# Two layers behind a linear attention: the second layer's weight loads planned as landing later, the weights' type change all on VectorE, first queries and keys loaded ahead of the first values

## The chip, the core and the metric

The program runs on one core of one Trainium2 chip. A time is the device time of one execution in microseconds (us), and of several runs the median. The engines are named as in the profile: PE (TensorE, the matmuls), DVE (VectorE), ACT (ScalarE), POOL (GpSimd; here it only issues DMAs that add to what lies in memory) and SP (SyncE, which issues all other DMAs, in order, each when what it waits for is done).

## The reference

Linear attention with decay over 2 batches, 8 heads, 768 positions of 64 values, and behind it two feed-forward layers on 1536 tokens (512 to 2048 to 512), the first with h·relu6(h+3)/6, the second with h·tanh(softplus(h)). All in fp32.

```python
for t in range(S):
    state = gamma * state + einsum('bhd,bhe->bhde', k[:, :, t], v[:, :, t])
    y[:, :, t] = scale * einsum('bhd,bhde->bhe', q[:, :, t], state)
x = y.transpose(0, 2, 1, 3).reshape(B * S, H * D)
h = x @ w_in;  g = h * clip(h + 3, 0, 6) / 6;    x = g @ w_out      # first layer
h = x @ w_in;  g = h * tanh(log1p(exp(h)));      out = g @ w_out    # second layer
```

## The kernel before, in words

**The work.** The attention goes by 12 units (6 chunks of 128 positions, 2 batches). A unit loads `qk` (queries and keys, 512 KB) and `kv` (keys, values and decay factors, 516 KB). On PE it has scores `sc`, the state's update `kv`, what the state gives `qv`, and what the chunk itself gives `pv`. Before `kv` the keys are multiplied by decay factors: `kp`, on DVE in one instruction (L600) or on ACT in eight (L598), as the letter of the unit in `KPD` says. The scores are multiplied by a mask (L612), which is made once from two tables (matmuls that read the loaded `rows`, tile `cvd`) and a triangle (`tri`) in L429; ACT copies five more tables to `qtab` (L435).

A layer is computed transposed, features on partitions and 512 tokens at a time, in three blocks. A product of fp32 accuracy is three passes of PE in its faster fp32 form: each operand is split into a high and a low part (high on ACT, L483 or L893; low on DVE, L485 or L895), and high·high, low·high and high·low are added in PSUM. Where pairs of blocks are multiplied, seven products stand for eight (as Strassen's do): the up products are named P1 to P7, of two blocks of tokens (`w`) or of the halves of one (`v`); DVE adds their sums in PSUM to what ACT copied (L850; the plan calls these c11, c12, c22), and a later product (P4) uses the bank that such an addition (c22) has read.

**The weights.** They lie in memory as 64-bit words. For each pair of feature tiles there are two loads of 1 MB (`raw`, L454): up weights (converted into tile `cvu`) and down weights (`cvd`). Of the two `raw` buffers a third load can take one only when the first has been converted. A conversion is four instructions, one behind the other: a shift (L468), a shift-and-or (L469), a mask (L471), and the top part, a change from fp32 to fp16 with a factor 0.5. This last one is on ACT (L474) or on DVE (L476), as the letter in `TOPS` says, two conversions a letter (first eight letters: the first layer's pairs; last eight: the second's). So ACT makes 24 of them before, each of 128x1024.

**The second layer's sums.** Products of different pairs of features are added in memory: the first time by a plain write from SP (L981, tile `part`), later by DMAs from POOL that add (L983).

**What sets the order.** Everything is first a list of tasks (`Plan.add`) with an engine, a duration, and what it depends on. `Plan.order` plays them through with the table of costs at the top of the file, and issues them in the order in which that play has them start; each engine then runs its own instructions strictly in that order, whatever the real times. `EARLY` gives the order of PE's attention tasks (s, k, q, b) and of the first layer's first up (h) and down (o) tasks; `LOADS` the first six loads. `Plan.lat` is what the plan adds after the end of a task before its successors may start: `DLAT` for what SP issues, 0.06 otherwise. `Plan.ranks` counts back from the tasks that PE needs, with the same latencies. So a larger latency for a load has two effects: its rank asks for it earlier, and the instructions that read it are placed later among their engine's others.

Of the kernel before, what the change touches and what calls it, by code (L numbers as in the profile page):

```python
# [44 lines left out]
LAT = 0.06  # L45
# [2 lines left out]
SC, KV, QV, PV = 0.86, 0.43, 0.42, 0.84  # L48
TURN = 0.15
LEAD = (7.2, 5.5)  # L50
EARLY = "bskbskkbbkqssqssbkqsqsqqkbskqkksqbbhqobqskbobhhhohohhohhshoohoooboho"
LOADS = "kv0 qk0 kv1 tri qk1 rows"
DLAT = 1.45
OUT = 4.0
COLD = 9.0
EARLY_Y = (1, 2, 5, 6, 3, 7, 4)
# [3 lines left out]
ORDER = (1, 5, 6, 3, 7, 2, 4)  # L60
AFTER = ("bp", "bp", "bp", "pb")
BORDER = {"pb": (2, 3, 0, 1), "bp": (0, 1, 2, 3)}
TOPS = "DDDDAAAAAAAAAAAA"
KPD = "ADDADDDADA"


def dve(n, two=True):
    return 0.15 + n * (1.045e-3 if two else 0.525e-3)


def act(n, bias=False):
    return 0.17 + n * 0.86e-3 + (0.09 if bias else 0.0)
# [30 lines left out]
class Plan:  # L103
# [3 lines left out]
    def add(self, nm, eng, dur, deps, bufs, emit, rank=None):  # L107
        bufs = list(dict.fromkeys(getattr(b, "base", b) for b in bufs))
        t = Task(nm, eng, dur, deps, bufs, emit, rank)
        t.idx = len(self.tasks)  # L110
        self.tasks.append(t)
        for b in bufs:
            if not b.users:
                t.new.append(b)
                b.owner = t
            elif b.owner not in t.deps:
                t.deps.append(b.owner)
            b.users.append(t)
        for d in t.deps:
            d.succ.append(t)  # L120
        return t

    @staticmethod
    def lat(d):
        return DLAT if d.eng == "SP" else LAT

    def ranks(self):
        for t in reversed(self.tasks):
# [79 lines left out]
def body(ctx: ExitStack, tc: tile.TileContext, aps: dict, out: bass.AP):  # L208
# [17 lines left out]
    def buf(pool, shape, tag, dt=F32):  # L226
        count[0] += 1
        name = f"{tag}_{count[0]}"

        def make():  # L230
            if pool == "post" and "post" not in pools:
                att.close()
                pools["post"] = ctx.enter_context(tc.tile_pool(name="post", bufs=1, reuse_waits="tile"))
            return pools[pool].tile(shape, dt, tag=tag, name=name, bufs=BUFS.get(tag, 1))
        return Buf(tag, make)
# [7 lines left out]
    V, A = nc.vector, nc.scalar  # L243
    pl = Plan()
    add = pl.add
# [26 lines left out]

    first = LOADS.split()
    cst, tri_b = buf("fix", [P, 1024], "cvd"), buf("att", [P, P], "tri")
# [98 lines left out]
    hq = i = 0  # L373
    for c in EARLY:
        if c in "skqb":
# [68 lines left out]
    def words_of(layer, p, half, cb, parts):  # L444

        rb = buf("fix", [P, 1024], "raw", I64)
        src = aps["w1" if layer == 0 else "w2"][p, half]

        def part(k):
            n = 1024 // parts  # L450
            cs = slice(k * n, (k + 1) * n)
            nm = f"w{layer}_{p}_{half}{k}"
            ld = add(nm, "SP", DMA512 * n / 512, [], [rb],
                     lambda: nc.sync.dma_start(out=rb.tile[:, cs], in_=src[:, cs]))  # L454
            ld.after = ld_w[0]
            ld_w[0] = ld

            def words():
                w = rb.tile.bitcast(I32).rearrange("p (n t) -> p n t", t=2)
                return w[:, cs, 0], w[:, cs, 1]  # L460

            def ci():
                return cb.tile.bitcast(I32)[:, cs]

            def top():
                return cb.tile.bitcast(F16).rearrange("p (n t) -> p n t", t=2)[:, cs, 1]
            a1 = add(nm + "l", "DVE", dve(n, False), [ld], [rb, cb],
                     lambda: V.tensor_scalar(ci(), words()[0], 29, None, ALU.logical_shift_right))  # L468
            a2 = add(nm + "o", "DVE", dve(n), [a1], [cb, rb], lambda: V.scalar_tensor_tensor(  # L469
                out=ci(), in0=words()[1], scalar=3, in1=ci(), op0=ALU.logical_shift_left, op1=ALU.bitwise_or))  # L470
            a3 = add(nm + "m", "DVE", dve(n, False), [a2], [rb], lambda: V.tensor_scalar(  # L471
                words()[1], words()[1], -0x2000, None, ALU.bitwise_and))
            if TOPS[8 * layer + p] == "A":
                return add(nm + "t", "ACT", act(n), [a3], [cb, rb], lambda: A.activation(  # L474
                    top(), words()[1].bitcast(F32), AF.Copy, scale=0.5))
            return add(nm + "t", "DVE", dve(n, False), [a3], [cb, rb], lambda: V.tensor_scalar(  # L476
                top(), words()[1].bitcast(F32), 0.5, None, ALU.mult))
        return part

# [96 lines left out]
    def unit(u):  # L576
# [15 lines left out]
        if c < NCH - 1:  # L592
            kpb = buf("att", [P, DM], "kp")

            def run_kp():
                for h in range(H):
                    hs = slice(h * D, (h + 1) * D)
                    A.activation(kpb.tile[:, hs], kb.tile[:, hs], AF.Copy, scale=kb.tile[:, 2 * DM + h:2 * DM + h + 1])  # L598
            if KPD[u] == "D":
                t_kp = add(f"kp{u}", "DVE", DVE1, [ld_kv[u]], [kb, kpb], lambda: V.tensor_tensor(  # L600
# [626 lines left out]
```

## Time and profile before

| | |
|---|---|
| median of 3 runs | 548.85 us (548.23 to 549.57) |
| profiled execution: its time, its span | 550.77 us, 549.0 us |
| PE busy | 537.0 us of the span |
| DVE busy | 441.2 us |
| ACT busy | 330.2 us |
| chain that ended last | PE 94%, DMA 3%, ACT 1%, issue 1% |

How to read the rows below: a time at the start of a row is in us from the start of the span. `out<-in` are tile names without their numbers; `x3` counts instructions. A bracket at a row's end is the idle time of the engine ahead of the instruction and what ended it. Granted clock 1.00 is PE at 2.4 GHz and 0.50 at 1.2 GHz. PE's matmuls overlap: one of 128x512 lasts 0.39 us, and one starts 0.227 us after the other when nothing holds them.

### The profile page before, as it was taken

Reading aid. Unit: us, or ns where it says so; the run is one execution under the profiler, and the core shown is the slowest. Engines: PE = TensorE matmul, PEld = TensorE weight load, DVE = VectorE, ACT = ScalarE, POOL = GpSimd, SP = SyncE. Lnnn points to the kernel's source line nnn. Section 1 sums busy time; section 2 is a strip of 40 time slices with the busy share of each in tenths; the row PEclk is TensorE's granted clock in tenths of the full one; section 3 lists DMA queues with packets and bytes.
Section 4 is the critical chain, followed back from the end, with each engine's and each line's share of the span. In section 5 each row is a group of like instructions: output and inputs, shape, how many; then the busy total and the mean of one; then the engine's idle time right before and its main releaser. Section 6 shows DMA issues by size and latency. Waiting matters only on the chain.

```text
span 549.0 us, 8237 instructions
## 1 busy us (share of the span) xinstructions
PE 537.0 (98%) x3142; PEld 452.5 (82%) x3143; DVE 441.2 (80%) x716; ACT 330.2 (60%) x572; POOL 31.9 (6%) x40
## 2 busy tenths in 40 slices
PE   7999999999999999999999999998999999999996
PEld 4888888888889988888888898876988898888985
DVE  3999999599746994678999989956899778878592
ACT  4666453566724644457655787764868776867440
POOL 0000000000000000000000000010023300540000
PEclk9999999999999999999999999997999999999999
DMA  8985522122400242003130023392259942995232
GB/s 310 369 289 205 214 83 92 72 77 78 153 1 1 76 155 77 1 5 137 35 133 0 1 88 141 116 266 80 78 123 191 190 111 76 146 143 173 79 127 102
DMA packets 19111, 65.79 MB, mean 120 GB/s; under 512 B 2128, under 2 KB 2512, under 8 KB 15232
## 3 DMA queue, kind: packets, MB, share of 16 engines
q1 hardware_dynamic: 13888, 55.83, 28.2%
q0 software_dynamic: 5184, 9.44, 11.7%
q8 instruction: 24, 0.39, 0.3%
q14 instruction: 15, 0.12, 0.1%
HBM read 49.53 MB, written 15.73 MB: 119 GB/s over the span
## 4 chain that ended last, share of the span: by engine, by line
PE 94%; DMA 3%; ACT 1%; issue 1%; DVE 0%; SPq 0%; DVEq 0%; ACTq 0%
PE acc L241 49%; PE wx L241 24%; PE wy L241 21%; DMA raw<-in_w_dram 2%; DMA qk<-in_qk_dram 1%; ACT cvd L474 0%; DVE g L850 0%; ACT qc L674 0%; ACT wbh L483 0%; SPq L260 0%; DVE cvu L468 0%; ACT sb L972 0%; ACT qc L972 0%; ACT t L972 0%; DVE xch L975 0%
## 5 line engine op out<-in xcount | busy, mean ns | idle before, releaser
L241 PE MATMUL acc<-gh,wdh 128*128 128x512 f32 x264 | 103.1, 390 | 0.0
L241 PE MATMUL acc<-gh,wdl 128*128 128x512 f32 x264 | 103.0, 390 | 0.0
L241 PE MATMUL acc<-gl,wdh 128*128 128x512 f32 x264 | 102.7, 389 | 0.0
L241 PEld LDWEIGHTS acc<-gl,wdh 128*128 128x128 f32 x264 | 49.6, 188 | 10.4
L241 PEld LDWEIGHTS acc<-gh,wdh 128*128 128x128 f32 x264 | 49.6, 188 | 9.8 <-issue 0.2
L241 PEld LDWEIGHTS acc<-gh,wdl 128*128 128x128 f32 x264 | 49.6, 188 | 9.3
L893 ACT CAST gh<-g 128x512 fp32r<-128x512 f32 x56 | 34.8, 621 | 28.9 <-PE acc L241 23.7
L895 DVE TENSOR_TENSOR gl<-g,gh 128x512 fp32r<-128x512 f32 x56 | 38.4, 687 | 15.3 <-ACT gh L893 12.9
L983 POOL DMA_DIRECT2D part<-sb x18 | 15.9, 955 | 440.2 <-ACT sb L972 426.1
L895 DVE TENSOR_TENSOR gl<-gs,gh 128x512 fp32r<-128x512 f32 x29 | 20.0, 688 | 12.2 <-ACT gh L893 11.2
L485 DVE SCALAR_TENSOR_TENSOR wdl<-cvd,wdh 128x512 fp32r<-128x512 f32 x32 | 21.7, 686 | 9.9 <-ACT wdh L483 9.7
L763 ACT ACTIVATE t<-g,bias 128x512 f32<-128x512 f32 (+1 forms) x22 | 14.6, 664 | 24.0 <-DVE g L850 21.0
L241 PE MATMUL acc<-gh,sb 128*128 128x512 f32 x92 | 28.3, 389 | 0.0
L893 ACT CAST gh<-gs 128x512 fp32r<-128x512 f32 x29 | 18.0, 621 | 14.6 <-PE acc L241 14.3
L483 ACT ACTIVATE wdh<-cvd 128x512 fp32r<-128x512 f32 x32 | 20.0, 637 | 6.9 <-PE acc L241 6.8
L531 DVE TENSOR_TENSOR cvu<-cvu 128x256 f32<-128x256 f32 x56 | 23.5, 420 | 0.5
L471 DVE TENSOR_SCALAR raw<-raw 128x1024 int32<-128x1024 int32 (+1 forms) x34 | 22.3, 657 | 0.0
L241 PE MATMUL wy<-xbh,wsh 128*128 128x512 f32 x56 | 22.3, 398 | 0.0
L241 PE MATMUL wy<-xbh,wsl 128*128 128x512 f32 x56 | 22.3, 398 | 0.0
L241 PE MATMUL wx<-q,wsh 128*128 128x512 f32 x56 | 21.8, 389 | 0.0
L850 DVE TENSOR_TENSOR g<-wy,g 128x512 f32<-128x512 f32 (+1 forms) x26 | 14.6, 564 | 8.5 <-PE wy L241 8.1
L485 DVE SCALAR_TENSOR_TENSOR wsl<-cvu,wsh 128x1024 fp32r<-128x1024 f32 x14 | 17.1, 1222 | 4.5 <-ACT wsh L483 4.4
(248 smaller groups left out, 1509.0 us busy)
## 6 DMA issues: line engine op xcount, KB each, us to landing
raw<-in_w_dram SPq DMA_DIRECT2D x30, 1024.0 KB, 4.8
kv<-in_kv_dram SPq DMA_DIRECT2D x12, 516.0 KB, 6.0
qk<-in_qk_dram SPq DMA_DIRECT2D x12, 512.0 KB, 6.3
part<-sb POOLq DMA_DIRECT2D x18, 256.0 KB, 5.0
raw<-in_w_dram SPq DMA_DIRECT2D x4, 512.0 KB, 9.4
part<-q POOLq DMA_DIRECT2D x8, 256.0 KB, 5.6
part<-sb SPq DMA_DIRECT2D x6, 256.0 KB, 2.1
part<-t POOLq DMA_DIRECT2D x5, 256.0 KB, 5.4
```

The source lines that it names most:

```text
L241: nc.tensor.matmul(o, l, r, start=start, stop=stop, skip_group_check=True)
L471: a3 = add(nm + "m", "DVE", dve(n, False), [a2], [rb], lambda: V.tensor_scalar(words()[1], words()[1], -0x2000, None, ALU.bitwise_and))
L483: lambda: A.activation(hb.tile[:, h0:h0 + n], cb.tile[:, c0:c0 + n], AF.Copy, scale=256.0))
L485: return add(nm + "lo", "DVE", dve(n), [a], list(dict.fromkeys([cb, hb, lb])), lambda: V.scalar_tensor_tensor(out=lb.tile[:, l0:l0 + n], i ...
L531: prev = [add(nm + f"s{o}", "DVE", dve(256), prev, [cb], lambda o=o, x=x, y=y, op=op: V.tensor_tensor(out=q(o), in0=q(x), in1=q(y), op=op))]
L763: lambda: A.activation(tb.tile[:, cs], src.tile[:, cs], AF.Relu, bias=bias3))
L850: return add(f"c{k}_{nm}", "DVE", dve(n), deps, [ps, gb], lambda: V.tensor_tensor(out=gb.tile[:, gc], in0=ps.tile[:, pc], in1=gb.tile[:, g ...
L893: a = add(f"hi{nm}", "ACT", act(512), deps + [prev_split[0]], [gb, gh], lambda: A.copy(gh.tile, gb.tile))
L895: lambda: V.tensor_tensor(out=gl.tile, in0=gb.tile, in1=f32(gh.tile), op=ALU.subtract))
L983: landed[tp] = added[b, d] = add(f"pa{nm}", "POOL", ADDED, [dep, added[b, d]], [tp, pt], lambda: nc.gpsimd.dma_start(out=pt.tile, in_=tp.t ...
```

## The change

Three things in the tables and rules of the plan; no instruction's own work is changed.

- `Plan.lat` gives the loads of the second layer's weights (task names that begin with `w1_`) 7.0 us to land instead of 1.45. All other loads keep 1.45.
- `TOPS` is `D` throughout: the 24 type changes that were on ACT are on DVE. The planned cost of one is 1.1 times the plan's formula on DVE (it was 1.0), and 1.33 times on ACT, where none is left.
- `EARLY` and `LOADS` are new, and one letter of `KPD`: the first loads are `rows`, `tri`, `qk` of unit 0, `kv` of units 0 and 1, `qk` of unit 1; `kp` of unit 6 is made on ACT in eight instructions instead of on DVE in one.

```diff
-EARLY = "bskbskkbbkqssqssbkqsqsqqkbskqkksqbbhqobqskbobhhhohohhohhshoohoooboho"
-LOADS = "kv0 qk0 kv1 tri qk1 rows"
-DLAT = 1.45
+EARLY = "bkssksqssqksbbkkqbkbsqbsqkqbkqksqkbhqbqsshobbhhohhhhkooosoohoohhboooh"
+LOADS = "tri rows qk0 kv0 kv1 qk1"
+DLAT, WLAT = 1.45, 7.0
...
-TOPS = "DDDDAAAAAAAAAAAA"
-KPD = "ADDADDDADA"
+TOPS = "DDDDDDDDDDDDDDDD"
+KPD = "ADDADDAADA"
...
-        return DLAT if d.eng == "SP" else LAT
+        return (WLAT if d.nm[:3] == "w1_" else DLAT) if d.eng == "SP" else LAT
...
-                return add(nm + "t", "ACT", act(n) * 1.33 ...
+...
```

Since the plan is played anew, every engine's order shifts. Two places are shown, before and after.

**The start, SP.** The first loads that SP issues, before (`kv_78` and `qk_85` are unit 0, `kv_87` and `qk_89` unit 1):

```order
L281 DMA cvd_76<-in_rows_dram 48x704
L260 DMA kv_78<-in_kv_dram 128x1032
L260 DMA tri_83<-in_tri_dram 128x128
L260 DMA qk_85<-in_qk_dram 128x1024
L260 DMA kv_87<-in_kv_dram 128x1032
L260 DMA qk_89<-in_qk_dram 128x1024
```

And now (`qk_83` and `kv_85` are unit 0):

```order
L281 DMA cvd_76<-in_rows_dram 48x704
L260 DMA tri_78<-in_tri_dram 128x128
L260 DMA qk_83<-in_qk_dram 128x1024
L260 DMA kv_85<-in_kv_dram 128x1032
L260 DMA kv_87<-in_kv_dram 128x1032
L260 DMA qk_89<-in_qk_dram 128x1024
```

The first values have gone from second place to fourth, the triangle and the first queries and keys are each one place further ahead. `rows` stays first.

**The start, ACT.** Its first instructions after loading its table, before: the decayed keys of unit 0 (eight), then the tables, then the first copies of the state (`st`).

```order
L598 ACTIVATE kp_103<-kv_78 128x64 x8
L435 COPY qtab_133<-wy_99 128x512
L435 COPY qtab_135<-wx_112 128x512
L435 COPY qtab_137<-acc_40_118 128x512
L435 COPY qtab_139<-acc_41_121 128x512
L624 COPY st_156<-acc_34_80 128x512
```

And now:

```order
L435 COPY qtab_110<-wy_101 128x512
L435 COPY qtab_114<-wx_106 128x512
L435 COPY qtab_118<-acc_40_112 128x512
L435 COPY qtab_130<-acc_41_116 128x512
L598 ACTIVATE kp_132<-kv_85 128x64 x8
L435 COPY qtab_150<-acc_42_145 128x512
```

Four tables have moved ahead of `kp`, which waits for the values.

**The second layer's first sums, DVE.** The instructions around the first one that reads the up weights of the second layer's pair 4 (`cvu<-raw`, L468), before; the L850 rows are the additions c11, c12 and c22 of pair 2's up products:

```order
L850 TENSOR_TENSOR g_739_3530<-wy_3586,g_739_3530 128x512
L485 SCALAR_TENSOR_TENSOR wdl_3608<-cvd_3370,wdh_3599 128x512
L468 TENSOR_SCALAR cvu_3611<-raw_3566 128x1024
L850 TENSOR_TENSOR g_740_3595<-wy_3557,g_740_3595 128x512
L531 TENSOR_TENSOR cvd_3370<-cvd_3370 128x256
L850 TENSOR_TENSOR g_742_3582<-wx_3409,g_742_3582 128x512
```

And now (the L850 rows of 128x256 are the additions of the next set of products, pair 2's `v`):

```order
L850 TENSOR_TENSOR g_740_3604<-wy_3573,g_740_3604 128x512
L485 SCALAR_TENSOR_TENSOR wdl_3630<-cvd_3460,wdh_3618 128x512
L850 TENSOR_TENSOR g_742_3592<-wx_3545,g_742_3592 128x512
L485 SCALAR_TENSOR_TENSOR wdl_3648<-cvd_3460,wdh_3627 128x512
L531 TENSOR_TENSOR cvd_3460<-cvd_3460 128x256 x4
L850 TENSOR_TENSOR wsh_753_3582<-wy_3661,wsh_753_3582 128x256
L850 TENSOR_TENSOR wsh_753_3582<-wy_3633,wsh_753_3582 128x256
L485 SCALAR_TENSOR_TENSOR sb_263_3678<-cvd_3460,sb_263_3678 128x1024
L468 TENSOR_SCALAR cvu_3698<-raw_3580 128x1024
L850 TENSOR_TENSOR wsh_753_3582<-wx_3559,wsh_753_3582 128x256
```

The reader of the load stood between c11 and c12 of pair 2; it now stands behind all three of them, behind two of the next set, the sums of the down weights (L531) and their split (L485).

**The same place, SP.** The load that this reader waits for is `raw_274`; before:

```order
L981 DMA part20_331_3484<-sb00_696_3325 128x512
L981 DMA part21_332_3491<-sb01_697_3334 128x512
L454 DMA raw_265_3515<-in_w2_dram 128x1024
L454 DMA raw_274_3566<-in_w2_dram 128x1024
L981 DMA part12_329_3570<-q_695_3406 128x512
L981 DMA part13_330_3574<-q_695_3406 128x512
```

And now:

```order
L981 DMA part20_331_3475<-sb00_696_3328 128x512
L981 DMA part21_332_3486<-sb01_697_3338 128x512
L981 DMA part12_329_3552<-q_695_3411 128x512
L981 DMA part13_330_3556<-q_695_3411 128x512
L454 DMA raw_265_3569<-in_w2_dram 128x1024
L454 DMA raw_274_3580<-in_w2_dram 128x1024
```

The two loads now stand behind the two writes of sums that followed them.

## Rows read from the trace of the kernel before

**Rows 1.** The page's first part: busy time, share of the span, instructions

```profile
PE 537.0 (98%) x3142; PEld 452.5 (82%) x3143; DVE 441.2 (80%) x716; ACT 330.2 (60%) x572; POOL 31.9 (6%) x40
```

**Rows 2.** Waits of PE: in total, times, longest (us)

```profile
PE wx L241 <- DVE g L850: 4.0, 1, 4.0
PE wy L241 <- DMA qk<-in_qk_dram: 2.0, 1, 2.0
```

**Rows 3.** Timeline of PE around its longest wait: start, duration, instruction

```profile
368.87 0.39 PE L241 MATMUL wx<-xal,wbh 128*128 128x512 f32 x1
373.23 0.80 PE L241 MATMUL wx<-t4h,wbh 128*128 128x512 f32 x1 [3.98 <-DVE g L850]
...
378.93 0.39 PE L241 MATMUL wx<-t2h,wsl 128*128 128x512 f32 x1
```

**Rows 4.** Windows there: busy time of each engine, granted clock, DMA share

```profile
373.23:378.88 5.65, 5.65 (x13) 4.46 (x14) 2.69 (x5) 3.06 (x5) 0.00 (x0) 0.50 0.00 0
378.88:384.50 5.62, 5.62 (x27) 4.63 (x26) 3.93 (x5) 3.25 (x5) 0.00 (x0) 1.00 0.52 187
```

**Rows 5.** Timeline of DVE around PE's longest wait

```profile
370.95 0.69 DVE L468 TENSOR_SCALAR cvu<-raw 128x1024 int32<-128x1024 int32 x1 [4.20 <-DMA raw<-in_w_dram]
...
372.49 0.69 DVE L850 TENSOR_TENSOR g<-wx,g 128x512 f32<-128x512 f32 x1
```

**Rows 6.** The chain that ended last, there: start, us, what

```profile
361.85 9.01 DMA raw<-in_w_dram
```

**Rows 7.** Timeline of SP there: two issues, from the first to the second's end

```profile
356.92 5.27 SPq L454 DMA_DIRECT2D raw<-in_w_dram  x2
```

**Rows 8.** Timeline of POOL there, first and last of four

```profile
355.94 1.01 POOL L983 DMA_DIRECT2D part<-sb  x1 [355.49 <-ACT sb L972]
...
360.90 1.23 POOL L983 DMA_DIRECT2D part<-qc  x1
```

**Rows 9.** The page's DMA issues: times, KB each, median us to landing

```profile
raw<-in_w_dram SPq DMA_DIRECT2D x30, 1024.0 KB, 4.8
```

**Rows 10.** A group of instructions by form: busy, mean ns of one, idle before

```profile
L474 ACT ACTIVATE cvu<-raw 128x1024 f16<-128x1024 f32 x12 | 16.6, 1386 | 0.8 <-DVE raw L471 0.7
```

**Rows 11.** Instructions of L476: duration ns min/median/max, first and last start

```profile
L476 DVE TENSOR_SCALAR cvu<-raw x5: 458/756/760, 19.1 to 93.8; 128x1024 f16<-128x1024 f32 x3, 128x512 f16<-128x512 f32 x2
```

**Rows 12.** A window where DVE is full, columns as in rows 4

```profile
290.00:310.00 20.00, 19.99 (x88) 16.23 (x87) 20.00 (x34) 12.74 (x22) 0.00 (x0) 1.00 0.00 0
```

**Rows 13.** Timeline of PE at the start

```profile
5.17 1.06 PE L241 MATMUL acc<-cvd 48*128 48x512 bf16 x2
8.27 0.55 PE L241 MATMUL wy<-qk 64*128 64x128 f32 x1 [2.04 <-DMA qk<-in_qk_dram]
...
9.04 0.42 PE L241 MATMUL wy<-qk 64*128 64x128 f32 x1
...
9.26 0.42 PE L241 MATMUL wy<-qk 64*128 64x128 f32 x1
...
10.28 1.12 PE L241 MATMUL acc<-kv,kp 128*64 128x64 f32 x16
...
13.01 0.63 PE L241 MATMUL wy<-qk 64*128 64x128 f32 x2
...
15.72 0.27 PE L241 MATMUL wy<-qk 64*128 64x128 f32 x1
...
15.84 0.27 PE L241 MATMUL wy<-qk 64*128 64x128 f32 x1
...
18.05 0.43 PE L241 MATMUL acc<-qs,st 64*64 64x128 f32 x2
```

**Rows 14.** Timeline of ACT and DVE at the start: what the first loads release

```profile
4.58 2.02 ACT L598 ACTIVATE kp<-kv 128x64 f32<-128x64 f32 x8 [2.56 <-DMA kv<-in_kv_dram]
...
4.82 0.69 DVE L429 TENSOR_TENSOR mask<-wy,tri 128x512 f32<-128x512 f32 x1 [3.38 <-DMA tri<-in_tri_dram]
```

**Rows 15.** The chain that ended last, at the start

```profile
2.12 6.02 DMA qk<-in_qk_dram
```

More of the change, by code (lines that the diff above doesn't have):

```diff
@@ L50 @@
 LEAD = (7.2, 5.5)
-EARLY = "bskbskkbbkqssqssbkqsqsqqkbskqkksqbbhqobqskbobhhhohohhohhshoohoooboho"
-LOADS = "kv0 qk0 kv1 tri qk1 rows"
-DLAT = 1.45
+EARLY = "bkssksqssqksbbkkqbkbsqbsqkqbqksqkbhqbqsshobbhhohhhhkooosoohoohhboooh"
+LOADS = "tri rows qk0 kv0 kv1 qk1"
+DLAT, WLAT = 1.45, 7.0
 OUT = 4.0
@@ L473, in part @@
             if TOPS[8 * layer + p] == "A":
-                return add(nm + "t", "ACT", act(n), [a3], [cb, rb], lambda: A.activation(
+                return add(nm + "t", "ACT", act(n) * 1.33, [a3], [cb, rb], lambda: A.activation(
                     top(), words()[1].bitcast(F32), AF.Copy, scale=0.5))
-            return add(nm + "t", "DVE", dve(n, False), [a3], [cb, rb], lambda: V.tensor_scalar(
+            return add(nm + "t", "DVE", dve(n, False) * 1.1, [a3], [cb, rb], lambda: V.tensor_scalar(
                 top(), words()[1].bitcast(F32), 0.5, None, ALU.mult))
```

## The prediction

> **What bounds the kernel now.** I read the page's busy times first, then PE's waits, then the places that these named in the timeline. PE is busy 537.0 of 549.0 us [rows 1]: what does not shorten PE's idle time, or raise its clock, is worth nothing. Its waits hold two entries of any size [rows 2]: 4.0 us once, for an addition on DVE, and 2.0 us once, for the first queries and keys. The 4.0 us are in the second layer: no matmul starts between 368.87 and 373.23 [rows 3]. DVE is named as the releaser, but DVE itself stood still there for 4.20 us, waiting for a weight load [rows 5]; PE's addition (L850, 372.49) was queued behind that load's first reader, with which it has nothing to do. The load took 9.01 us from issue to landing [rows 6], where the median of its kind is 4.8 [rows 9]. In these 9 us POOL's four adding DMAs, issued from 355.94 on [rows 8], shared the DMA engines with it and with the 1 MB load issued 4.9 us ahead of it [rows 7].
>
> The stall costs twice. For 5.65 us behind it PE's granted clock is 0.50, the lower of its two levels, and 13 matmuls take what 27 do at 1.00 [rows 4]. From 368.87 to 378.93 there are 14 steps from one matmul to the next [rows 3]; at 0.227 us each they need 3.2 us. So 10.06 - 3.2 = 6.9 us went there: 4.1 standing, 2.8 on the clock.
>
> **The change, part by part.**
>
> *The longer landing time.* It takes the reader of that load (L468) out of the way. DVE came to it at 366.75 (370.95 less the wait, [rows 5]), just behind c11 of pair 2. In the new order it stands behind c12, c22 and two additions of the `v` products, so PE does three more products of 512 columns and four of 256 first: 18 x 0.227 + 24 x 0.12 (half of 0.227, and some) = 7.0 us, and DVE the 128x1024 split behind them, some 1.2 us. DVE asks at about 375. SP issues both loads together, when the conversions ahead are done, now on DVE: about 362 to 363, for the second load was already issued at 361.85, when ACT had finished the same conversion. That is 12 to 13 us of room. Landing: at best twice 2.6 us of transfer and some 2 us beside it (4.8 less 2.6), 7 us; at worst the 9.01 us of before and the other load's 2.6 us ahead of it, 11.6. It lands in time by either end, though by only half a microsecond or so at the worst. Gain 6.9 us; both ends are kept (6.9, or a stall of a few us left over). Past it, the second layer's other loads landed within the times that the old order allowed, since PE's waits name no other; the new order asks for all of them later after their issue.
>
> The two loads are also moved behind two SP writes of 256 KB. These wait for ACT's copies of the last products' sums, finished at about the same time as the conversions; cost 0, at worst 1 us off the room above.
>
> The Trainium skill ("DMA: Bandwidth & Descriptors", Queues, rings and completion order) says that each DMA engine takes turns, packet by packet, between the queues that have work for it. The trace agrees as far as it goes: 9.01 us beside POOL's queue, 4.8 without. By that rule two loads in one queue share one turn; with all of POOL's four still running they would take 2 x 5.1 us and 2 of latency, 12.2, at the edge of that room.
>
> *The type change on DVE.* 24 x 0.756 = 18.1 us are added to DVE's 441.2 [rows 1, 11] and 24 x 1.386 = 33.3 us leave ACT (12 of them have the row in [rows 10], the 12 for `cvd` take the same). Neither is on the chain: DVE goes from 80% to 84% of the span. What hides it is DVE's own idle time, 549 - 441 = 108 us. Where there is none it would show: from 290 to 310 DVE is busy for all of 20 us, and PE still never waits [rows 12]. The new order moves no conversion into that stretch. A chain of a conversion gets shorter (0.756 for 1.386, and no change of engine), so the third load of each trio is issued sooner. I take 0; below, nothing but a few tenths of small waits can be gained; above, 18.1 us if nothing hid it.
>
> *The start.* PE's tables end at 6.2 (5.17 + 1.06), then it waits until 8.27 for the first queries and keys [rows 13], issued fourth [rows 15]. Now they are third behind 196 KB. In before, the first values and the triangle were at hand at 4.58 and 4.82 [rows 14], and the bytes up to there are the same; so they can be there at 4.8 and the scores start at 6.2, 2.0 us sooner. But the next PE task of weight is `kv` of unit 0. It needs the values, now in fourth place, thus at about 8.1 (2.12 + 6.02), then ACT's 2.02 us [rows 14]: 10.2, where before it started at 10.28 [rows 13]. PE is idle for a microsecond or more ahead of it. The gain is in what no longer stands behind it. Before, from 10.28 to 18.05 PE did two more units' scores, three updates, two `pv` and two small tasks; now the small ones, some 0.6 us with the gap around them, are done in the wait, and the rest has 7.1 us from 10.2 on: 17.3, a gain of 0.7. The scores' steps were 0.22 us at 9.04, two of 0.42 us still take 0.63 at 13.01, and at 15.72 the steps are 0.12 [rows 13]: PE ran at half speed to somewhere behind 13.4; I take 13.6, so 3.3 of these us. If it is at full speed from 10.2, half of these go too: 2.3. If the new idle time puts the rise off by 2 us, 1.0 is lost: -0.3. If the values land at 7 rather than 8.1, one more is gained. I take 1.3, between -0.3 and 3.3.
>
> The Trainium skill ("TensorE: Matmul & The Clock Gate", Part 1) says the lower clock is the default, and that sustained activity releases it. By it the new start, with scores straight behind the tables, reaches the upper clock earlier than 13.6, and the sum would have 2.3. The trace only shows activity of 2 us to 6.2 followed by idle and then a slow start; it doesn't decide.
>
> *The `kp` of unit 6* leaves DVE (0.69, as the mask's instruction of 128x512, [rows 14]) and is 2.02 us on ACT, like unit 0's [rows 14], beside PE's attention work. Cost 0, at worst 0.6, one update's matmuls.
>
> **Sum.** Against the profiled execution: 549.0 - 6.9 - 1.3 = 540.8 us of span, with 1.8 around it (550.77 - 549.0) 542.6. The median of the runs, 548.85, lies 0.15 below the span; so 540.7 for the median.
>
> **Rivals.**
>
> *The stall comes back* (loads land too late). For: the room is 12 to 13 us, the bounds reach 11.6, and two writes stand ahead. Against: DVE's new order has no addition of pair 2's `w` products behind the reader. Price: each us too late is one of DVE; up to 4 us standing and, if PE stops that long, the 2.8 of the clock: 543 to 547.6.
>
> *The start gains nothing* or loses 0.3: 542.0 to 542.3. For: `kv` of unit 0 can't start earlier. Against: the scores are out of its way.
>
> *The start gains all*, 2.3 to 3.3: 539.7 to 538.7.
>
> *DVE becomes the bound, and the kernel is slower.* In order, a type change stands ahead of an addition for which PE waits, with nothing to fill: at 84% of the span, in stretches that are full. Each of the 24 costs up to 0.756. It decides from the point where 8.2 of the 18.1 us show at PE, 0.34 us per change; all of it would give 540.7 + 18.1 = 558.8, with half 549.7. For: DVE full in [rows 12]. Against: there PE waits nowhere, 108 us are idle, and ACT, for which DVE waits too, has 33 us less.
>
> *The change does not do what it says*: the new plan puts another reader ahead of its load, a stall like the one removed in another place: 548.85 - 1.3 = 547.6.
>
> **How the numbers follow.** The forecast, 540.7, has 0.62 with its own range of 538.9 to 543; the full start 0.12 (539); no gain at the start 0.10 (542.2); the stall in part or whole, here or elsewhere, 0.11 (543 to 547.6); DVE the bound 0.05 (549 and over). The range, 538.5 to 546, leaves out DVE and the worst of the stall. A difference under 0.2%, 1.1 us, can't be told from none here: faster needs under 547.75. The stall that comes back whole ends on that edge, so faster 0.92, same 0.04, slower 0.04.
>
> **What would show it.** PE's waits without the 4.0 us entry and the granted clock at 1.00 through the second layer; DVE's longest wait for a weight load under 1 us; L476 with 34 instructions and about 459 us of DVE busy; ACT near 299. At the start, the first scores at about 6.2, `kv` of unit 0 near 10.2, the first `qv` at 16 to 17.5. PE's busy time should fall by some 3 us, its clock's share of the gain. It would be wrong if DVE waits for a load with PE behind it, or if PE's waits name L476 or an addition behind one.

## The result, and the profile after

The changed kernel takes 542.8 us (median of 4 runs, 542.6 to 543.88) beside 549.21 of the kernel before (4 runs, 548.23 to 550.1); the ratio is 0.9888, 95% interval [0.9865, 0.991], a gain of 6.2 us (4.9 to 7.4). Forecast were 540.7 and a gain of 8.2. The profiled execution has a span of 542.0 us. (In the diff above the new `EARLY` is misprinted: behind `bkssksqssqksbbkkqbkbsqbsqkqb` it goes on `qksqkbh`, with no `k` between.)

The page's first part, to be read beside [rows 1]:

```profile
PE 532.2 (98%) x3143; PEld 449.8 (83%) x3143; DVE 454.7 (84%) x739; ACT 306.7 (57%) x556; POOL 33.3 (6%) x40
```

PE is busy 4.8 us less, DVE 13.5 us more, ACT 23.5 us less. PE's waits (in total, times, longest), which answer to [rows 2]:

```profile
PE wy L241 <- DMA qk<-in_qk_dram: 3.1, 3, 1.6
PE acc L241 <- DVE t L411: 1.5, 1, 1.5
PE wy L241 <- ACT g L847: 0.7, 1, 0.7
```

The 4.0 us entry is gone. Two are new: three waits for queries and keys instead of one, and 0.7 us for a copy on ACT. The 1.5 us for `t` stand ahead of PE's first matmul, in the kernel before as well. The same stretch as in the first line of [rows 4], with its columns:

```profile
373.23:378.88 5.65, 5.65 (x29) 4.79 (x28) 5.65 (x8) 3.33 (x6) 0.00 (x0) 1.00 0.00 0
```

PE begins 29 matmuls there, at granted clock 1.00, where it began 13 at 0.50. DVE in the same place (compare [rows 5]), and below it the two loads, each row a DMA issue with its size and the us from issue to landing:

```profile
368.89 0.68 DVE L850 TENSOR_TENSOR g<-wx,g 128x512 f32<-128x512 f32 x1
...
373.33 1.22 DVE L485 SCALAR_TENSOR_TENSOR sb<-cvd,sb 128x1024 fp32r<-128x1024 f32 x1
374.46 0.68 DVE L468 TENSOR_SCALAR cvu<-raw 128x1024 int32<-128x1024 int32 x1
```

```profile
raw<-in_w_dram SPq DMA_DIRECT2D x1, 1024.0 KB, 6.6
...
raw<-in_w_dram SPq DMA_DIRECT2D x1, 1024.0 KB, 8.3
```

The second row is the load for L468. It still takes 8.3 us. It was issued at 362.00 and so landed 4.2 us before L468 asked, at 374.46; c22 (368.89), for which PE waited before, is now ahead of L468.

The start, PE (compare [rows 13]), then ACT's `kp` of unit 0 (compare [rows 14]), then PE's waits for queries and keys:

```profile
5.96 0.42 PE L241 MATMUL wx<-qk 64*128 64x128 f32 x1
6.03 0.42 PE L241 MATMUL wy<-qk 64*128 64x128 f32 x1
6.17 0.44 PE L241 MATMUL wx<-qk 64*128 64x128 f32 x1
...
8.84 1.06 PE L241 MATMUL acc<-kv,kp 128*64 128x64 f32 x16
...
10.92 0.27 PE L241 MATMUL wy<-qk 64*128 64x128 f32 x1
10.93 0.27 PE L241 MATMUL wx<-qk 64*128 64x128 f32 x1
11.03 0.27 PE L241 MATMUL wy<-qk 64*128 64x128 f32 x1
...
15.10 0.77 PE L241 MATMUL acc<-qs,st 64*64 64x128 f32 x16
```

```profile
6.90 2.04 ACT L598 ACTIVATE kp<-kv 128x64 f32<-128x64 f32 x8
```

```profile
18.50 0.34 PE L241 MATMUL wy<-qk 64*128 64x128 f32 x1 [1.60 <-DMA qk<-in_qk_dram]
21.06 0.34 PE L241 MATMUL wy<-qk 64*128 64x128 f32 x1 [0.81 <-DMA qk<-in_qk_dram]
...
46.53 0.34 PE L241 MATMUL wy<-qk 64*128 64x128 f32 x1 [0.71 <-DMA qk<-in_qk_dram]
```

The first `qv` starts at 15.10 instead of 18.05. Scores step by 0.21 us into one bank at 6 us and by 0.11 at 11; before, they still took 0.21 a step at 13. Read as the clock, PE is at its upper level by 11 now and was not at 13 before. That is read from the steps alone: the granted clock in the profile's rows is 1.00 from 5 to 16 us in both kernels. After 15.10 PE waits 1.6, 0.8 and 0.7 us for queries and keys.

### The profile page after: what moved, and what is told of

Read it like the earlier page. It is cut to its first block, busy times and chain, and to the rows that moved or that the text cites. A ratio compares the mean times of both kernels' runs of the same rounds, so it can differ in the third digit from the quotient of the medians.

```text
span 542.0 us, 8217 instructions
## 1 busy us (share of the span) xinstructions
PE 532.2 (98%) x3143; PEld 449.8 (83%) x3143; DVE 454.7 (84%) x739; ACT 306.7 (57%) x556; POOL 33.3 (6%) x40
## 4 chain that ended last, share of the span: by engine, by line
PE 95%; DMA 3%; DVE 1%; issue 0%; ACT 0%; DVEq 0%; ACTq 0%
PE acc L241 49%; PE wx L241 25%; PE wy L241 21%; DMA qk<-in_qk_dram 3%; DVE kp L600 0%; DVE A L612 0%; DVE qs L608 0%; ACT g L847 0%; DVE t L411 0%; DVE xch L975 0%; DVEq L1222 0%; DVE xcl L679 0%; DVE bias L222 0%; DVEq L608 0%; ACTq L847 0%
## 5 line engine op out<-in xcount | busy, mean ns | idle before, releaser
L241 PEld LDWEIGHTS acc<-gl,wdh 128*128 128x128 f32 x264 | 49.6, 188 | 10.5
L983 POOL DMA_DIRECT2D part<-sb x18 | 17.1, 1133 | 433.5 <-ACT sb L972 421.7
L895 DVE TENSOR_TENSOR gl<-gs,gh 128x512 fp32r<-128x512 f32 x29 | 19.9, 686 | 10.5 <-ACT gh L893 9.6
L763 ACT ACTIVATE t<-g,bias 128x512 f32<-128x512 f32 (+1 forms) x22 | 14.6, 664 | 23.5 <-DVE g L850 22.2
L485 DVE SCALAR_TENSOR_TENSOR wdl<-cvd,wdh 128x512 fp32r<-128x512 f32 x32 | 21.4, 684 | 4.3 <-ACT wdh L483 4.2
L531 DVE TENSOR_TENSOR cvu<-cvu 128x256 f32<-128x256 f32 x56 | 23.4, 418 | 0.4
L850 DVE TENSOR_TENSOR g<-wy,g 128x512 f32<-128x512 f32 (+1 forms) x26 | 14.7, 565 | 10.4 <-PE wy L241 9.8
L847 ACT COPY g<-wx 128x512 f32<-128x512 f32 (+1 forms) x26 | 12.7, 487 | 15.2 <-PE wx L241 14.7
## 6 DMA issues: line engine op xcount, KB each, us to landing
raw<-in_w_dram SPq DMA_DIRECT2D x4, 512.0 KB, 10.2
```

Source lines behind the costliest of these rows:

```text
L241: nc.tensor.matmul(o, l, r, start=start, stop=stop, skip_group_check=True)
L485: return add(nm + "lo", "DVE", dve(n), [a], list(dict.fromkeys([cb, hb, lb])), lambda: V.scalar_tensor_tensor(out=lb.tile[:, l0:l0 + n], i ...
L531: prev = [add(nm + f"s{o}", "DVE", dve(256), prev, [cb], lambda o=o, x=x, y=y, op=op: V.tensor_tensor(out=q(o), in0=q(x), in1=q(y), op=op))]
L763: lambda: A.activation(tb.tile[:, cs], src.tile[:, cs], AF.Relu, bias=bias3))
L847: lambda: A.copy(gb.tile[:, gc], ps.tile[:, pc]))
L850: return add(f"c{k}_{nm}", "DVE", dve(n), deps, [ps, gb], lambda: V.tensor_tensor(out=gb.tile[:, gc], in0=ps.tile[:, pc], in1=gb.tile[:, g ...
```

## The experiments

Each was timed in alternation with the kernel before; its ratio is to that kernel in the same set. A per cent is 5.5 us.

**1. Longer landing alone** (on the kernel before).

```diff
-DLAT = 1.45
+DLAT, WLAT = 1.45, 7.0
-        return DLAT if d.eng == "SP" else LAT
+        return (WLAT if d.nm[:3] == "w1_" else DLAT) if d.eng == "SP" else LAT
```

> The kernel before with one part of the change: the second layer's weight loads planned with 7.0 us to land. Theory A (the prediction's: this part is what takes the stall away): in the new order the reader of pair 4's load (L468) stands behind c12 and c22 of pair 2, so the 4.0 us wait of PE and the half clock behind it go, 6.9 us: 549.2 - 6.9 = 542.3 us; the start stays as before (first qv at 18.05). Theory B (the type change on DVE is what moved that reader, the longer landing only seemed to): the stall stays, or most of it, 547 to 549.2 us.

Measured: 543.18 us, ratio 0.9898 [0.9872, 0.9925], 5.6 us gained (4.1 to 7.0). Theory A holds in its mechanism, with 1.3 us less than its 6.9; PE's waits have only the start left:

```profile
PE wy L241 <- DMA qk<-in_qk_dram: 2.0, 1, 2.0
PE acc L241 <- DVE t L411: 1.5, 1, 1.5
```

**2. Type change alone** (on the kernel before).

```diff
-TOPS = "DDDDAAAAAAAAAAAA"
+TOPS = "DDDDDDDDDDDDDDDD"
```

(and the two factors of the planned costs.)

> The kernel before with one part of the change: all type changes on DVE, landing time and start as before. Theory A (the prediction's: the type change costs nothing and gains nothing, the stall is the landing time's affair): 549.2 us, PE's 4.0 us wait still there. Theory B: the planned order of this kernel already has the reader of pair 4's load behind c22 of pair 2 and a split; in the changed kernel DVE ended that split at 370.17 and the load landed at 370.27, so DVE would wait some 0.1 us and PE not at all: 549.2 - 6.9 = 542.3, plus the new 0.7 us wait for ACT's copy at the layer switch, 543.0 us. Theory C (18.1 us more of DVE show at PE): above 549.2 us.

Measured: 545.93 us, ratio 0.9942 [0.9921, 0.9962], 3.2 us gained (2.1 to 4.3). Neither A nor C; B's mechanism with half of its gain. At pair 4 the reader is out of the way, as B said: L468 waits there for 0.88 us, behind c22, and PE has no wait. But a stall of the same kind has come up at a later pair of weights. DVE's wait there, and pieces of the chain that ended last (start, us, what):

```profile
371.04 0.69 DVE L468 TENSOR_SCALAR cvu<-raw 128x1024 int32<-128x1024 int32 x1 [0.88 <-DMA raw<-in_w_dram]
...
424.37 0.69 DVE L468 TENSOR_SCALAR cvu<-raw 128x1024 int32<-128x1024 int32 x1 [2.83 <-DMA raw<-in_w_dram]
```

```profile
412.17 11.75 DMA raw<-in_w_dram
...
424.37 0.69 DVE cvu L468
...
429.87 0.61 DVE g L850
...
430.52 1.66 PE wx L241 x6
```

That load took 11.75 us; DVE, held up by it, came late with the additions (L850), and PE stood 1.51 us for one of them at 430.52. With the 0.7 us for ACT's copy, which this kernel has too, that is 2.2 us of PE.

**3. The start alone** (on the kernel before): the lines of `EARLY`, `LOADS` and `KPD`.

> The kernel before with one part of the change: the new first loads, the new order of attention tasks and kp of unit 6 on ACT. Theory A (the prediction's term for the start): 549.2 - 1.3 = 547.9 us. Theory B (read off the changed kernel: the first qv is 2.95 us earlier, but PE then waits for queries and keys behind other loads, 1.6, 0.8 and 0.7 us): 549.2 - 0.4 = 548.8 us, with those three waits. Either way PE's 4.0 us wait in the second layer stays.

Measured: 548.59 us, ratio 0.9981 [0.9966, 0.9996], 1.0 us gained (0.2 to 1.9). Theory A's size. PE's waits for queries and keys come to 1.4 us here, not 3.1:

```profile
PE wx L241 <- DVE g L850: 3.4, 1, 3.4
...
PE wy L241 <- DMA qk<-in_qk_dram: 1.4, 2, 0.8
```

So the 3.1 us of the first profile are partly that execution's own.

**4. The changed kernel without the longer landing.**

```diff
-DLAT, WLAT = 1.45, 7.0
+DLAT, WLAT = 1.45, 1.45
```

> The changed kernel with the landing time of the second layer's loads put back to 1.45 us; type change and start as changed. Theory A (the longer landing takes the stall away): the stall comes back, 549.2 less 0.4 to 1.3 of the start, 547.9 to 548.8 us. Theory B (the type change on DVE alone already moves the reader far enough): as the changed kernel, 542.8 us, and DVE waits for that load by a few tenths at most.

Measured: 545.19 us, ratio 0.9925 [0.9902, 0.9948]. Between the two: the stall does not come back whole, but some 2 us of the changed kernel's gain are gone. DVE waits for pair 4's load again, which took 10.74 us here and 8.91 in run 2, and for the one of the later pair:

```profile
372.10 0.69 DVE L468 TENSOR_SCALAR cvu<-raw 128x1024 int32<-128x1024 int32 x1 [2.45 <-DMA raw<-in_w_dram]
...
424.14 0.69 DVE L468 TENSOR_SCALAR cvu<-raw 128x1024 int32<-128x1024 int32 x1 [1.56 <-DMA raw<-in_w_dram]
```

```profile
PE wx L241 <- ACT gs L847: 0.8, 1, 0.8
```

Both loads are in the chain that ended last. Behind the first, ACT stands 3.74 us for an addition on DVE, and PE 0.82 us for the ACT copy that comes next (0.20 us more for an addition); behind the second PE stands 0.24. So the type change by itself moves the reader of pair 4 behind c22, but not far enough for every landing: 8.91 us cost PE nothing (run 2), 10.74 about 1 us. The longer landing is needed beside it, at pair 4 and at the later pair.

**5. Longer landing and start, without the type change**: the diffs of 1 and 3 together.

> The changed kernel without the type change: longer landing and new start, TOPS as before. Theory A (once the loads have a longer landing, the type change on DVE gains nothing more): the two parts add up as measured singly, 0.9898 and 0.9981 of before, 0.9879, some 543 us, as fast as the changed kernel; no wait for ACT's copy (L847) at the layer switch, and no DVE wait for a weight load. Theory B (the shorter chain of a conversion and the 24 x 1.386 us taken from ACT are part of the gain): 544 us or above.

Measured: 542.71 us, ratio 0.9883 [0.9856, 0.9911]. Theory A: as fast as the changed kernel. No wait for L847 is left; of DVE's waits for weight loads there is one of 0.3 us, where none was expected. The page's first part:

```profile
PE 533.4 (99%) x3143; PEld 450.3 (83%) x3143; DVE 442.0 (82%) x715; ACT 331.7 (61%) x580; POOL 32.9 (6%) x40
```

Against the changed kernel's page, the 24 type changes take 25.0 us of ACT and put 12.7 us on DVE.

**6. The four adding DMAs left out** (on the kernel before; this kernel does not add two sums, so its output differs).

```diff
-            ... add(f"pa{nm}", "POOL", ..., lambda: nc.gpsimd.dma_start(
+            ... add(f"pa{nm}", "POOL", ..., lambda: None if nm[:4] in ("0_7_", "0_2_") else nc.gpsimd.dma_start(
```

> The kernel before without the four adding DMAs of POOL that were issued from 355.94 to 360.90 (two sums of the second layer's block 0 are not added, so the output differs there). Theory A (these four slow the weight load to 9.01 us): it lands in 4.8 us as its kind does elsewhere, at 366.7, when DVE asks for it at 366.75; PE's 4.0 us wait and the half clock go, 549.4 - 6.9 = 542.5 us. Theory B (the load is slow by itself, being the second of two in SP's queue): it still takes 8 to 9 us and the stall stays, 549 us.

Measured: 545.0 us, ratio 0.9921 [0.9893, 0.9949], 4.3 us gained. Theory A in its mechanism: the load lands after 5.7 us instead of 9.0, DVE waits 0.92 us for it instead of 4.20, and PE 0.7 instead of 4.0. It is not the 4.8 us expected. The chain, DVE's wait, and PE's:

```profile
361.46 5.73 DMA raw<-in_w_dram
```

```profile
367.29 0.70 DVE L468 TENSOR_SCALAR cvu<-raw 128x1024 int32<-128x1024 int32 x1 [0.92 <-DMA raw<-in_w_dram]
```

```profile
PE wx L241 <- DVE g L850: 0.7, 1, 0.7
```

**7. Two weight loads of the first layer held back** (on the changed kernel).

```diff
-    ld_w = [None]
+    ld_w, HOLD = [None], {"w0_0_10": ld_qk[4], "w0_1_00": ld_qk[11]}.get
-            ld.after = ld_w[0]
+            ld.after = HOLD(nm) or ld_w[0]
```

> The changed kernel, with two weight loads of the first layer held back on SP: the first half of pair 0's down weights until queries and keys of unit 4 are issued, pair 1's up weights until those of unit 11 are. Their readers ran at 36.7 (L471) and 49.0 us (L468) in the changed kernel. Theory A (the start's gain is given back because queries and keys land behind weight loads that nobody needs yet): PE's waits for qk, 3.1 us in three pieces, fall under 1 us, and the time by 1 to 2 us, to 541 to 542 us. Theory B (the loads fill the DMA engines anyway, so that whatever stands last is late, and PE waits for that instead): 542.8 us, within 0.5.

Measured: 543.37 us, ratio 0.9893 [0.9862, 0.9925]. Theory A is right on the waits for queries and keys and wrong on the time. B's time holds, to 0.6 us; what PE now waits for is other engines:

```profile
PE acc L241 <- ACT q L674: 1.1, 1, 1.1
PE wy L241 <- DMA qk<-in_qk_dram: 0.7, 2, 0.5
...
PE acc L241 <- DVE qs L608: 0.3, 1, 0.3
```

Queries and keys come in time (0.7 us for 3.1), but PE now waits 1.1 us for a copy on ACT and 0.3 for DVE, and DVE 2.6 us for the load that was held back. The plan also put the attention tasks in another order; how much of the loss is that was not tried.

**8. The same two held back, with landing and start and the old type change.**

> Longer landing, new start and the two loads held back, type change as before the change. Theory A (landing and start carry the gain, the queue's order takes some of the start's away): 541 to 542 us, 1 us or more under the kernel with landing and start alone. Theory B (the order of the start's loads decides nothing): as the kernel with landing and start alone, some 543 us.

Measured: 543.02 us, ratio 0.9887 [0.9858, 0.9915]. Theory B again.

**9. A longer landing for one load** (on the kernel before).

```diff
-DLAT = 1.45
+DLAT, WLAT = 1.45, 7.0
...
-        return DLAT if d.eng == "SP" else LAT
+        return (WLAT if d.nm == "w1_4_00" else DLAT) if d.eng == "SP" else LAT
```

> The kernel before with 7.0 us to land for a single load, pair 4's up weights (w1_4_00), instead of for all of the second layer's. Theory A (the whole gain of the longer landing is that one reader's place on DVE): as the kernel with the longer landing alone, 0.990 of before, 543 us, no half clock. Theory B (other loads need it as well): the stall or a part of it shows at another load, 545 to 549 us.

Measured: 542.89 us, ratio 0.988 [0.986, 0.9901], 6.6 us gained (5.4 to 7.7). Theory A: that one reader's place is worth as much as the whole change. PE's waits are those of the start:

```profile
PE wy L241 <- DMA qk<-in_qk_dram: 1.7, 1, 1.7
PE acc L241 <- DVE t L411: 1.5, 1, 1.5
```

It is the reader's place and not the load: SP issues this load some 5 us behind the other one, as before, and it still takes 8.3 us. DVE asks later, and does not wait:

```profile
raw<-in_w_dram SPq DMA_DIRECT2D x1, 1024.0 KB, 8.3
```

```profile
371.43 0.69 DVE L468 TENSOR_SCALAR cvu<-raw 128x1024 int32<-128x1024 int32 x1
```

**10. The type changes twice** (on the changed kernel; the plan does not know of the second).

```diff
-            ..., lambda: V.tensor_scalar(
-                top(), words()[1].bitcast(F32), 0.5, None, ALU.mult))
+            ..., lambda: [V.tensor_scalar(
+                top(), words()[1].bitcast(F32), 0.5, None, ALU.mult) for _ in range(2 if 8 * layer + p > 3 else 1)])
```

> The changed kernel with each of the 24 type changes that had been on ACT issued twice on DVE (the second writes the same values), 24 x 0.756 = 18.1 us more of DVE; the plan's costs, and so all orders, as in the changed kernel. Theory A (such work is hidden in DVE's idle time, which is why the type change cost nothing): within 0.5 us of the changed kernel, 542.3 to 543.5 us. Theory B (in order, additions that PE waits for stand behind some of them, up to 0.756 us each): above 544 us; 0.34 us each would be 551.

Measured: 549.31 us, ratio 1.0001 [0.9985, 1.0016]; the changed kernel in the same set, run 11, had 0.9886. So 6.3 us more, 0.26 us for each of the 24, a third of their 18.1: theory B. One of the places, DVE and then PE:

```profile
439.21 0.68 DVE L850 TENSOR_TENSOR gs<-wy,gs 128x512 f32<-128x512 f32 x1
439.81 1.56 DVE L476 TENSOR_SCALAR cvd<-raw 128x1024 f16<-128x1024 f32 x2
441.25 0.68 DVE L850 TENSOR_TENSOR gs<-wy,gs 128x512 f32<-128x512 f32 x1
441.84 1.54 DVE L476 TENSOR_SCALAR cvu<-raw 128x1024 f16<-128x1024 f32 x2
443.27 0.67 DVE L850 TENSOR_TENSOR gs<-wx,gs 128x512 f32<-128x512 f32 x1
```

```profile
444.00 0.50 PE L241 MATMUL wx<-t4h,wbh 128*128 128x512 f32 x1 [1.27 <-DVE gs L850]
```

The three additions of a set (c11, c12, c22) have a doubled type change in each gap, and PE's P4 stands 1.27 us for the last one.

**11. The changed kernel again.**

> The changed kernel once more, beside the others. Both theories: 0.989 of before, some 543 us. Its profile tells whether the 3.1 us for which PE waited for queries and keys in the first profile are the rule, or whether 1.0 to 1.5 us are, as in the other kernels with the new start.

Measured: 543.08 us, ratio 0.9886 [0.9866, 0.9906], as the first time. PE's waits:

```profile
PE wy L241 <- DMA qk<-in_qk_dram: 2.1, 2, 1.3
...
PE wy L241 <- ACT g L847: 0.7, 1, 0.7
```

The wait for ACT's copy is the same in both profiles; that for queries and keys is 2.1, between the 3.1 of the first and the 1.4 of run 3.

**12. The one load and the start.**

> The two parts that the runs so far credit: 7.0 us to land for the one load of pair 4's up weights, and the new start; type change and all other landing times as before the change. Theory A (the two add, and nothing else in the change is needed): 0.988 x 0.998 = 0.986 of before, 541.5 us, some 1.5 us under the changed kernel. Theory B (the start's gain is not there any more beside the rest): 0.988, 543 us, as the changed kernel.

Measured: 542.54 us, ratio 0.9891 [0.9864, 0.9918]. Theory B: it is as fast as the changed kernel and not faster. No kernel tried here beats the changed one by more than the runs can tell.

## Why the prediction was right, and where it was not

*The stall* (-6.9). Right in place and in mechanism. The reader was moved behind c12 and c22, the 4.0 us and the half clock [rows 3, 4] are gone, and alone it is worth 5.6 us (run 1) or 6.6 (run 9); on the difference to 6.9 see *The size*. The room was worked out well: DVE asked at 374.46 (forecast 375), the loads were issued at 361.24 and 362.00 (362 to 363), the second landed after 8.3 us (7 to 11.6). In the second profile of the changed kernel it took 10.7, so the upper bound was no idle caution. (The 2.6 us of transfer in these bounds has no row beside it in the prediction. The 402 to 435 GB/s that the trace of before shows from 10.5 to 13.5 us give 2.4 to 2.6 for 1 MB.) The reason for the 9.01 us, POOL's adding DMAs, was argued in the prediction and is shown by run 6, for 3.3 of the 4.2 us above the usual.

The Trainium skill ("DMA: Bandwidth & Descriptors", Queues, rings and completion order) says that each DMA engine takes turns between the queues with work; by that rule the second load was to take 12.2 us. Where both loads were issued close together with POOL's queue at work, it took 8.3, 10.7 and, at the later pair in run 2, 11.75. The trace agrees in direction only. The full figure was not reached, and POOL's queue did not stay full: in the changed kernel it had 93.0% of the DMA engines' time from 362.1 to 362.9, none from 362.9 to 365, and 28.6% from 365 to 370.

*Whose merit it was.* Here the prediction's account was wrong. It gave the whole stall to the longer landing and nothing to the type change. But the type change alone takes 3.2 us (run 2), the landing alone 5.6, the one load 6.6, and both parts together no more than the landing (run 5 beside the changed kernel). They are two ways to move the same reader, and are not added; the longer landing moves it far enough alone, the type change does not (run 4). The order of each part by itself would have shown the first of this: in run 2's, L468 already stands behind c22.

*The type change* (0). The sum came out (run 5 beside the changed kernel), the working behind it was too simple. "What hides it is DVE's own idle time, 549 - 441 = 108 us": in run 10 the same work once more, with 87 us of idle time left, costs 6.3 us, 0.26 us for each, not far under the 0.34 at which the rival (DVE becomes the bound) was to decide. So idle time in the sum does not hide such work by itself; where it stands in the order decides. That the first 24 cost nothing because the plan knew of them and put additions ahead of them is the likely reason, but not shown: no run has the first 24 on DVE in an order made without them, and the second 24 came on top of a fuller DVE. The durations were also too large as terms: 24 x 0.756 = 18.1 us for DVE became 12.7, and 33.3 for ACT became 25.0 (run 5 beside the changed kernel). Instructions overlap their neighbours: in the rows above, one of 0.68 us is followed by the next after 0.60. At two neighbours each this gives 3.8 of the 5.4 us on DVE; the rest is open.

*The start* (-1.3). Alone 1.0 us (0.2 to 1.9), so the size stands, in part by luck: the working was off in two ways that cancel. The first `qv` came earlier than the 16 to 17.5 forecast, at 15.10. The values were there sooner: ACT began `kp` at 6.90, straight behind the tables and without waiting for a load, where 8.1 was forecast, and `kv` of unit 0 came at 8.84, not 10.2. And the short steps were reached earlier than the 13.6 that I took, by 10.92. Here the Trainium skill ("TensorE: Matmul & The Clock Gate", Part 1), by which sustained activity releases the upper clock, was the better guide: the steps were 0.11 us at 10.92, though the granted clock's rows do not show the change. But what came next was not asked: a PE that is 3 us ahead is ahead of its loads, which leave SP in one queue, and it waits 1.0 to 3.1 us for queries and keys in the profiles with the new start. Holding two other loads back (runs 7 and 8) only moved the wait.

*Not seen:* at the switch of the layers PE waits 0.73 us for a copy on ACT. P3 of the first pair stands there directly behind P5, whose bank that copy has to read first; this comes with the type change's order (it is in run 2 and not in run 5):

```profile
304.57 0.39 PE L241 MATMUL wy<-q,wsh 128*128 128x512 f32 x1
305.69 0.50 PE L241 MATMUL wy<-xbh,wsh 128*128 128x512 f32 x1 [0.73 <-ACT g L847]
```

*The size.* 8.2 us were forecast and 6.2 came. The terms that the runs give singly, 5.6 or 6.6 and 1.0, are together 6.6 to 7.6, each known to about 1 us; the 0.73 at the layer switch is on the other side. In the medians it can't be told (run 5, which lacks it, is no faster), and the start's 1.0 can't be seen beside the rest either (run 12 beside run 9).

About 1 us of the missing 2 lies in the clock's part of the stall, 2.8 of the 6.9 us. It was read from one execution and taken off the median. The 61 executions of the kernel before that were timed beside the experiments show that this part changes from one to the next, with no change in the program:

| mean granted clock | executions | median time, us |
|---|---|---|
| 0.994 | 25 | 550.0 |
| 0.996 or 0.997 | 28 | 549.1 |
| 0.999 | 8 | 547.4 |

The profiled execution, 550.77 us, had 0.994: 5.65 us at 0.50 and the 3.98 ahead of them at 0.85, in 549. The median execution is of the middle kind and pays 0.9 us less. Kernels without the stall (all but run 3's) had 0.998 to 1.000 in 75 of 78 executions. Why the clock stays low for longer in one execution than in another is open. The other 1 us is not settled: the start's 0.3 (1.0 for 1.3) and the 0.73 at the layer switch would fill it, but neither can be told in the medians.

*The signs to look for.* No 4.0 us entry, clock at 1.00 and no wait of DVE for a weight load: as forecast. PE busy fell by 4.8 us (forecast 3). The first scores start at 5.58 (6.2). DVE 454.7 (459) and ACT 306.7 (299) miss, at least in part by the overlap told above.

## What to carry to other kernels

Where a plan sets the order, read the order of each part of a change by itself before giving it a share of the gain: two parts that move the same reader out of the way do not add up, and one load's planned landing time was worth here what the whole change brought. A share of idle time does not hide work by itself: added where additions stand in a row, a third of it showed, on an engine that is idle for a sixth of the span. A stall's price, read from one execution, can hold a part that other executions pay only in half or not at all: look at their spread before taking it off a median. And a start made faster is soon ahead of its own loads: look at the landing of the next ones before counting the gain.

## What the runs showed of the hardware

- A 1 MB weight load took 4.8 us in the median of 30 [rows 9], 5.7 with the four adding DMAs gone (run 6; the end of another load was still ahead of it and two writes of 256 KB behind it), 8.3 to 10.7 with them, and at a later pair, with other adding DMAs, 11.75 (run 2) and 10.84 (run 4).
- Of the waits in the second layer that were profiled, the granted clock was low after the longer ones only. After 4.0 us [rows 4] it was 0.50 for 5.65 us, and after 3.4 us (run 3) 0.70 in the mean over as long a stretch; after the 1.51 us of run 2 it stayed at 1.00. Run 3 and then run 2, from the matmul behind the wait on (columns as in [rows 4]):

```profile
371.39:377.04 5.65, 5.65 (x18) 4.48 (x19) 2.69 (x5) 4.01 (x6) 0.00 (x0) 0.70 0.14 22
```

```profile
430.52:436.17 5.65, 5.65 (x25) 4.66 (x26) 4.42 (x7) 3.81 (x6) 0.87 (x1) 1.00 0.91 211
```

- In the kernel before, the executions with a mean granted clock of 0.994 took 550.0 us and those with 0.999 547.4 (medians of 25 and 8): 2.6 us, where 2.8 on the clock were read off the one trace.
